# Attention step of a fused attention and MLP kernel: score matmuls placed around the output matmuls

## The chip, the cores and the metric

One core of a Trainium2 chip runs the whole program as a single launch. The metric is device time in microseconds (us): the median of three runs, 599.78 us before the change, with the runs between 599.56 and 600.16 us.

## The reference: what is computed

Chunked attention on 4 batches x 8 heads x 768 positions with a head size of 64, followed by a two-layer MLP on the 3072 rows of 512 that it gives. The core of it, cut:

```python
for c in range(nc):                       # chunks of 32 queries
    l_start, r_end = max(0, c*32 - 16), min(S, c*32 + 32 + 8)
    k_full = concat([mem_k, k[:, :, l_start:r_end]])     # 8 memory keys + window
    v_full = concat([mem_v, v[:, :, l_start:r_end]])
    a = softmax(q_c @ k_full.T / 8)
    out[:, :, chunk] = a @ v_full
x = out.transpose(0, 2, 1, 3).reshape(3072, 512)
h = x @ w_in                              # 512 -> 2048
g = max(h, 0) + alpha * min(h, 0)
return g @ w_out                          # 2048 -> 512
```

All of it is float32. The large products are made exact enough by splitting each operand into a high and a low part and doing three matmuls (low x high, high x low, high x high).

## The kernel before

**The MLP.** The 3072 rows are cut into seven blocks, the first four of 384 rows and the last three of 512. For each block and each of 16 slices f of the hidden layer, an *up* step (L723, 12 matmuls) fills one of two PSUM banks, `h0` or `h1` in turn. ScalarE (L732) and VectorE (L735 `bend`, L741, L745) then turn that bank into the high and low parts of g. A *down* step (L753) later adds the slice into the block's output banks. These up and down steps are nearly all of the work of PE, the engine of the matmuls.

**The attention.** A unit is a pair of heads of one batch over half of the sequence; there are 32. Units 0 to 7 are done by other code at the start. Units 8 to 31 are done in twelve pairs, spread over the MLP. The list `BEGIN` names the place (the number of the MLP slice) at which each pair starts: 20, 26, 31, 36, 42, 47, 53, 57, 63, 71, 79, 87. At each such place `attend` issues on PE

- the *outputs* of the pair before (`olds`): `value_products` (L438), 8 matmuls a unit, on the transposed weights `pt` and on `v_t`; a float32 matmul stands in the trace as two records, so 32 for a pair;
- the *scores* of the pair that begins (`news`): `head_products` (L337), 24 matmuls a unit, 96 records for a pair, in tiles of 64x32.

The scores of both new units lie in two banks, `s0` for the first heads and `s1` for the second heads; each bank holds columns of both units. When a bank is complete, VectorE masks it (L347 or L349), takes row maxima over both units at once (L360) and negates them (L363). ScalarE then does the exponentials (L371). Later VectorE transposes the weights into `pt` (L413), which the outputs of this pair will read one place later.

The outputs of a unit lie in one bank. `bank(u)` gives `a` to even units and `h1` to odd units below 24, but `h0` to even and `h1` to odd units from 24 to 29. From there ScalarE copies the high part (`xh`, L474) and VectorE computes the low part (`xl`, L477), which also sets the bank free. So an up step that comes next in `h0` or `h1` waits until VectorE has done `xl` of the unit that lay there.

**What sets the order.** Nothing is scheduled on the chip: each engine takes its instructions in the order in which the program holds them. That order is made when the program is built, by a planner (`Plan.send`). Each piece of work is a *step* with an engine, an assumed cost, the keys that it reads and writes (banks, tiles), and a due time. The planner runs a list schedule over them and emits each step's instructions when its turn comes. The assumed costs thus decide the order on all engines, and nothing else; waits on the chip come from real dependences.

Of the kernel before, what the change touches and what calls it, by code (L numbers as in the profile page):

```python
# [70 lines left out]
PE, DVE, ACT, POOL, SP = "PE", "DVE", "ACT", "POOL", "SP"  # L71
# [110 lines left out]
def body(ctx: ExitStack, tc: tile.TileContext, qvw, kw, first, w_in, w_out, alpha, out):  # L182
    nc = tc.nc
    ctx.enter_context(tc.manual_schedule())
    NKB, NPT, NA = 2, 2, 2
# [20 lines left out]
    qk = [const.tile([P, BT + NT * NKT], F32, name=f"qk{i}") for i in range(NKB)]  # L206
# [21 lines left out]
    step = plan.add  # L228
# [20 lines left out]
    def rest(place):  # L249
        wide = NNARROW * NF  # L250
        return (len(ORDER) - max(place, wide)) * WIDE_PAIR + max(wide - place, 0) * PAIR
# [9 lines left out]
    def sets(u):  # L261

        return u % NKB
# [55 lines left out]
    def banks(us):  # L319

        n = len(us)
        ss = [ps_s.tile([P, 512], F32, name="s_ps", tag=f"s{h2}")[:, :n * NJ * KW].rearrange("p (u n k) -> p u n k", u=n, n=NJ)
              for h2 in range(2)]
        for i, u in enumerate(us):
            state[u]["s"] = [s[:, i] for s in ss]
        state[us[0]]["all"] = ss

    def head_products(u):

        st = state[u]  # L330
        for n in range(NJ):
            for g in range(4):
                t, j = SLOT[(g, n)]
                c = t * NJ + j
                for h2 in range(2):
                    rows = slice(h2 * D, (h2 + 1) * D)
                    nc.tensor.matmul(  # L337
                        out=st["s"][h2][g * CH:(g + 1) * CH, n],
                        lhsT=qs[sets(u)][rows, c * CH:(c + 1) * CH],
                        rhs=kbs[sets(u)][rows, t, STARTS[j]:STARTS[j] + KW],  # L340
                        start=True, stop=True,
                    )
# [39 lines left out]
    def weights(u):  # L382
# [12 lines left out]
        def spread():  # L395
# [7 lines left out]
    TURNS = [(g, j, n0, n1, t0) + piece  # L403
             for g in range(4)
             for j, n0, n1, t0 in ([(g, 0, NJ, 0)] if g < NJ else [(n, n, n + 1, NT - 1) for n in range(NJ)])
             for piece in PIECES[j]]
# [15 lines left out]
    def bank(u):  # L422


        h2 = u % 2
        if u >= NU - 2:
            return ps_s, f"s{h2}", ("s", h2)
        if h2 or u >= 6 * NPAIR:
            return ps_h, f"h{h2}", f"h{h2}"
        return ps_a, "a", "a"  # L430

    def value_products(u):
        st = state[u]
        pool, tag, _ = bank(u)
        st["a"] = pool.tile([P, 512], F32, name="a_ps", tag=tag)
        for t in range(NT):
            for h2 in range(2):
                nc.tensor.matmul(  # L438
                    out=st["a"][h2 * D:(h2 + 1) * D, t * TQ:(t + 1) * TQ],
                    lhsT=st["v"][:, t, h2, :],  # L440
                    rhs=pts[u % NPT][:, :, t, h2, :],
                    start=True, stop=True,
                )

    def attend(place, olds, news):

        def outputs():
            for u in olds:
                value_products(u)

        def products():
            banks(news)
            for u in news:
                head_products(u)

        due_at = place + (0 if (olds + news)[-1] < FIRST_FRONT else 0.8 if news else -0.3)
        if olds:
            step(PE, 0.2 + 0.53 * len(olds), outputs,
                 reads=[x for u in olds for x in [("v", u % 2)] + [("pt", u % NPT, i) for i in range(len(TURNS))]],
                 writes=[bank(u)[2] for u in olds], rest=rest(due_at))  # L460
        if news:
            step(PE, 0.11 + 0.48 * len(news), products, reads=[(x, sets(u)) for u in news for x in "qk"],
                 writes=[("s", 0), ("s", 1)], rest=rest(due_at + 0.01))

    def split(u, ak="a"):

# [404 lines left out]
    for blk, f in ORDER:  # L871
        if blk == 0:
            decode(f)
        f0, f1 = (0, NF) if blk != 1 else (0, NJOINT) if f < NJOINT else (NJOINT, NF)
        add_up, add_bend, add_down = hidden(blk, f, f0, f1 - 1)
        add_up()
        if down is not None:
            down()
        if done is not None:
            done()  # L880
            done = None
        add_bend()
        now = todo.get(PLACE[blk, f], [])
        olds, news = ([u for u, part in now if part == which] for which in (2, 0))
        if olds or news:
            attend(PLACE[blk, f], olds, news)
        for u in olds:
            split(u, bank(u)[2])
            if u + 2 < NU:
                load_v(u + 2)  # L890
        for u, part in now:
            if part == 1:
                weights(u)
                turn(u)
        for u in news:
            unit_begins(u)
        o = o_ps.setdefault((blk, f1), [])
        down = partial(add_down, o)
        if f == f1 - 1:
            done = partial(keep if f1 < NF else store, blk, o)  # L900
# [57 lines left out]
```

## Time and profile before

| | |
|---|---|
| median of three runs | 599.78 us |
| lowest, highest | 599.56, 600.16 us |
| profiled execution: span from first to last instruction | 597.5 us |
| PE busy | 591.1 us (99%) |
| VectorE (DVE) busy | 386.7 us (65%) |
| ScalarE (ACT) busy | 210.6 us (35%) |
| granted TensorE clock | 1.000 |

The profiled execution is known by its span; its own time with what lies around the span is not recorded, and the median of the runs lies 2.3 us above the span. In the profile PE is the matmul row, PEld the weight loads of the same engine, DVE is VectorE and ACT is ScalarE. A line such as L337 is a line of the kernel before.

### The profile page before, as it was taken

Reading aid. Unit: us, or ns where it says so; the run is one execution under the profiler, and the core shown is the slowest. Engines: PE = TensorE matmul, PEld = TensorE weight load, DVE = VectorE, ACT = ScalarE, POOL = GpSimd, SP = SyncE. Lnnn points to the kernel's source line nnn. Section 1 sums busy time; section 2 is a strip of 40 time slices with the busy share of each in tenths; the row PEclk is TensorE's granted clock in tenths of the full one; section 3 lists DMA queues with packets and bytes.
Section 4 is the critical chain, followed back from the end, with each engine's and each line's share of the span. In section 5 each row is a group of like instructions: output and inputs, shape, how many; then the busy total and the mean of one; then the engine's idle time right before and its main releaser. Section 6 shows DMA issues by size and latency. Waiting matters only on the chain.

```text
span 597.5 us, 10975 instructions
## 1 busy us (share of the span) xinstructions
PE 591.1 (99%) x4430; PEld 505.7 (85%) x4430; DVE 386.7 (65%) x904; ACT 210.6 (35%) x580; POOL 36.5 (6%) x61
## 2 busy tenths in 40 slices
PE   8999999999999999999999999999999999999997
PEld 4789999888998989989898888888888888888885
DVE  5888898887959768685885852861862771530530
ACT  3788888644222504323233302302400411210201
POOL 3510000010001101010010100100100100000000
PEclk9999999999999999999999999999999999999999
DMA  8999500222040302403304003003101000000001
GB/s 337 359 399 407 226 0 1 66 65 89 2 152 2 101 23 79 153 1 100 94 8 150 4 1 100 2 0 109 62 2 36 1 0 36 36 1 0 1 1 71
DMA packets 21076, 48.96 MB, mean 82 GB/s; under 512 B 2464, under 2 KB 5792, under 8 KB 21024
## 3 DMA queue, kind: packets, MB, share of 16 engines
q1 hardware_dynamic: 20880, 48.12, 22.8%
q8 instruction: 35, 0.57, 0.4%
q14 instruction: 17, 0.14, 0.1%
q10 hardware_dynamic: 144, 0.13, 0.1%
HBM read 41.95 MB, written 6.29 MB: 81 GB/s over the span
## 4 chain that ended last, share of the span: by engine, by line
PE 96%; DMA 3%; SPq 0%; ACT 0%; issue 0%; ACTq 0%
PE h_ps L723 45%; PE o_ps L753 44%; PE a_ps L438 3%; DMA early<-first 3%; PE s_ps L337 2%; PE a_ps L559 1%; PE o_ps L546 1%; PE s_ps L312 0%; SPq L490 0%; PE o_ps L298 0%; ACT o_t L810 0%; PE s_ps L298 0%; ACTq L810 0%
## 5 line engine op out<-in xcount | busy, mean ns | idle before, releaser
L723 PE MATMUL h_ps<-xh,w 128*128 128x384 f32 (+1 forms) x896 | 248.8, 358 | 0.0
L723 PEld LDWEIGHTS h_ps<-xh,w 128*128 128x128 f32 x896 | 164.9, 188 | 16.0
L753 PE MATMUL o_ps<-w,gh 128*128 128x512 f32 x528 | 162.7, 389 | 0.0
L723 PE MATMUL h_ps<-xl,w 128*128 128x384 f32 (+1 forms) x448 | 162.6, 363 | 0.0
L732 ACT ACTIVATE g<-h_ps 128x384 f32<-128x384 f32 (+1 forms) x112 | 60.4, 540 | 194.7 <-PE h_ps L723 129.1
L735 DVE SCALAR_TENSOR_TENSOR g<-g,rise,h_ps 128x384 f32<-128x384 f32 (+1 forms) x112 | 74.7, 668 | 74.8 <-ACT g L732 74.1
L753 PEld LDWEIGHTS o_ps<-w,gh 128*128 128x128 f32 x528 | 99.1, 188 | 20.4
L413 DVE STREAM_TRANSPOSE pt<-e 32x64 f32<-32x64 f32 (+1 forms) x336 | 99.4, 301 | 7.4 <-POOL e L392 2.0
L753 PE MATMUL o_ps<-w,gl 128*128 128x512 f32 x264 | 102.8, 389 | 0.0
L723 PEld LDWEIGHTS h_ps<-xl,w 128*128 128x128 f32 x448 | 84.1, 188 | 10.2
L753 PE MATMUL o_ps<-w,xh 128*128 128x512 f32 x240 | 74.8, 393 | 0.0
L753 PEld LDWEIGHTS o_ps<-w,gl 128*128 128x128 f32 x264 | 49.6, 188 | 10.2
L477 DVE TENSOR_TENSOR xl<-a_ps,xh 128x384 fp32r<-128x384 f32 x32 | 17.6, 554 | 61.0 <-ACT xh L474 60.4
L753 PEld LDWEIGHTS o_ps<-w,xh 128*128 128x128 f32 x240 | 45.0, 188 | 8.9
L741 DVE CAST gh<-g 128x512 fp32r<-128x512 f32 (+1 forms) x72 | 28.8, 401 | 30.6 <-PE o_ps L753 28.2
L474 ACT CAST xh<-a_ps 128x384 fp32r<-128x384 f32 x32 | 15.0, 483 | 95.0 <-PE a_ps L438 93.7
L392 POOL TENSOR_TENSOR e<-e,den 128x384 f32<-128x384 f32 x24 | 22.8, 949 | 419.6 <-DVE den L389 270.0
L745 DVE TENSOR_TENSOR gl<-g,gh 128x512 fp32r<-128x512 f32 (+1 forms) x72 | 46.6, 648 | 1.7
L371 ACT ACTIVATE e<-s_ps,mx 128x64 f32<-128x64 f32 x144 | 43.4, 318 | 11.1 <-DVE mx L363 11.1
L753 PE MATMUL o_ps<-w,xl 128*128 128x512 f32 x120 | 46.8, 390 | 0.0
L371 ACT ACTIVATION_READ_ACCUMULATOR e<-s_ps,mx 128x1 f32 x144 | 30.4, 211 | 0.0
L810 ACT COPY o_t<-o_ps 128x512 f32<-128x512 f32 x21 | 12.2, 591 | 44.6 <-PE o_ps L753 44.2
(58 smaller groups left out, 380.2 us busy)
## 6 DMA issues: line engine op xcount, KB each, us to landing
w_t<-w_in SPq DMA_DIRECT2D x16, 512.0 KB, 10.0
w_t<-w_out SPq DMA_DIRECT2D x16, 512.0 KB, 10.1
qk<-kw SPq DMA_DIRECT2D x24, 272.0 KB, 4.3
v_t<-qvw SPq DMA_DIRECT2D x24, 256.0 KB, 2.8
out<-o_t SPq DMA_DIRECT2D x23, 256.0 KB, 2.1
early<-first SPq DMA_DIRECT2D x8, 656.0 KB, 6.2
qk<-qvw SPq DMA_DIRECT2D x24, 192.0 KB, 4.8
early<-first SPq DMA_DIRECT2D x8, 256.0 KB, 6.3
```

The source lines that it names most:

```text
L371: nc.scalar.activation(out=st["e"][:, i], in_=st["s"][h2][:, n], func=AF.Exp, scale=SCALE, bias=d["mx"][:, u - us[0], n, h2:h2 + 1], accum ...
L392: nc.gpsimd.tensor_tensor(out=st["e"], in0=st["e"], in1=st["den"].broadcast_to([P, NJ * 2, KW]), op=ALU.mult)
L413: nc.vector.transpose(out=pts[u % NPT][quad * CH:(quad + 1) * CH, j, t0:t0 + n1 - n0].rearrange("p t h q -> p (t h) q"), in_=(st["e"], zer ...
L438: nc.tensor.matmul(out=st["a"][h2 * D:(h2 + 1) * D, t * TQ:(t + 1) * TQ], lhsT=st["v"][:, t, h2, :], rhs=pts[u % NPT][:, :, t, h2, :], sta ...
L474: nc.scalar.copy(out=ring[k][0][:, cols], in_=st["a"][:, :BT])
L477: nc.vector.tensor_tensor(out=ring[k][1][:, cols], in0=st["a"][:, :BT], in1=ring[k][0][:, cols].bitcast(F32), op=ALU.subtract)
L723: nc.tensor.matmul(out=h["ps"][:, :n_cols], lhsT=ws[f, 0][:, wk, k * P:(k + 1) * P], rhs=parts(blk, k)[1](xk), start=(k == 0 and n == 0), ...
L732: nc.scalar.activation(out=h["g"], in_=h["ps"][:, :n_cols], func=AF.Relu, scale=-1.0)
L735: nc.vector.scalar_tensor_tensor(out=h["g"], in0=h["g"], scalar=rise[:, f:f + 1], in1=h["ps"][:, :n_cols], op0=ALU.mult, op1=ALU.add)
L741: copy(out=h["gh"], in_=h["g"])
L745: nc.vector.tensor_tensor(out=h["gl"], in0=h["g"], in1=h["gh"].bitcast(F32), op=ALU.subtract)
L753: nc.tensor.matmul(out=o_ps[tt], lhsT=h[gk][:, tt * P:(tt + 1) * P], rhs=ws[f, 1][:, wk], start=(f == first_f and i == 0), stop=(f == last ...
```

## The change

In a step that has both older and new units, outputs and scores were two separate planner steps. They become one step, `around`: scores of the first new unit, outputs of both older units, scores of the second new unit. The step reads and writes what both read and wrote. The assumed costs change too: 2.66 us for the joint step where the two had 1.26 and 1.07 us, and 1.68 and 1.27 us for outputs or scores that stand alone. Eleven places have such a joint step (all of `BEGIN` but the first); the first pair's scores and the last pair's outputs stay alone.

```diff
-        def products():
-            banks(news)
-            for u in news:
+        def products(us):
+            if us[0] == news[0]:
+                banks(news)
+            for u in us:
                 head_products(u)
+        def around():
+            products(news[:1])
+            outputs()
+            products(news[1:])
...
+        if olds and len(news) > 1:
+            step(PE, 1.0 + 0.83 * len(olds), around, reads=fed + asked, writes=made + scored, rest=rest(due_at))
+            return
         if olds:
-            step(PE, 0.2 + 0.53 * len(olds), outputs, ... rest=rest(due_at))
+            step(PE, 0.2 + 0.74 * len(olds), outputs, reads=fed, writes=made, rest=rest(due_at))
         if news:
-            step(PE, 0.11 + 0.48 * len(news), products, ... rest=rest(due_at + 0.01))
+            step(PE, 0.11 + 0.58 * len(news), partial(products, news), reads=asked, writes=scored, rest=rest(due_at + 0.01))
```

In the changed kernel the lines behind `attend` have numbers higher by 9: L477 becomes L486, L723 becomes L732, L753 becomes L762.

What it makes of the order, at three places. First PE at place 71, the first of three places (71, 79 and 87) whose outputs lie in `h0` and `h1`. `s_ps` are the scores, `a_ps` the outputs, `h_ps` the bank of the up step that follows; the words behind a row name the engines for whose semaphores it waits. Before:

```order
L753 MATMUL o_ps<-w,gh 128x512 x2
L438 MATMUL a_ps<-pt_634,v_t 64x96 [waits DMAHW7_49]
L438 MATMUL a_ps<-pt_634,v_t 64x96 x7
L438 MATMUL a_ps<-pt_636,v_t 64x96 [waits DMAHW0_49]
L438 MATMUL a_ps<-pt_636,v_t 64x96 x7
L337 MATMUL s_ps<-qk_154 32x64 x22
L337 MATMUL s_ps<-qk_155 32x64 [waits DMAHW4_49,DMAHW2_49]
L337 MATMUL s_ps<-qk_155 32x64 x23
L723 MATMUL h_ps<-xl,w 128x512 [waits DVE_49]
```

and now:

```order
L762 MATMUL o_ps<-w,gh 128x512 x2
L337 MATMUL s_ps<-qk_154 32x64 x22
L438 MATMUL a_ps<-pt_634,v_t 64x96 [waits DMAHW2_49]
L438 MATMUL a_ps<-pt_634,v_t 64x96 x7
L438 MATMUL a_ps<-pt_636,v_t 64x96 [waits DMAHW3_49]
L438 MATMUL a_ps<-pt_636,v_t 64x96 x7
L337 MATMUL s_ps<-qk_155 32x64 [waits DMAHW5_49,DMAHW1_49]
L337 MATMUL s_ps<-qk_155 32x64 x23
L732 MATMUL h_ps<-xl,w 128x512 [waits DVE_49,PE_49]
```

One unit's scores moved ahead of the outputs; between the outputs and the up step there is now one unit's scores instead of two. Second, VectorE at the same place (`MEMSET s_ps` is the mask, `TENSOR_REDUCE mx` the maxima, `xl<-a_ps` what sets `h0` and `h1` free). Before, and then now:

```order
L745 TENSOR_TENSOR gl<-g,gh 128x512
L477 TENSOR_TENSOR xl<-a_ps,xh 128x384 x2
L347 MEMSET s_ps 32x2x16
L360 TENSOR_REDUCE mx<-s_ps 128x6
L363 TENSOR_SCALAR mx<-mx 128x12
```

```order
L754 TENSOR_TENSOR gl<-g,gh 128x512
L347 MEMSET s_ps 32x2x16
L360 TENSOR_REDUCE mx<-s_ps 128x6
L486 TENSOR_TENSOR xl<-a_ps,xh 128x384 x2
L363 TENSOR_SCALAR mx<-mx 128x12
```

The mask and the maxima of the first score bank moved ahead of both `xl`. (The second bank's mask and maxima stand behind the `xl` rows in both, and their rows would read like the first's.) In the planner both are ready at the end of the one joint step, and the maxima have the earlier due time. Third, PE at place 26, where the two parts stood apart: before, the scores went first and the outputs came 18 us later, with up and down steps between.

```order
L337 MATMUL s_ps<-qk_154 32x64 x24
L337 MATMUL s_ps<-qk_155 32x64 x24
L723 MATMUL h_ps<-xl,w 128x384
...
L438 MATMUL a_ps<-pt_634,v_t 64x96 x8
L438 MATMUL a_ps<-pt_636,v_t 64x96 x8
```

```order
L337 MATMUL s_ps<-qk_154 32x64 x24
L438 MATMUL a_ps<-pt_634,v_t 64x96 x8
L438 MATMUL a_ps<-pt_636,v_t 64x96 x8
L337 MATMUL s_ps<-qk_155 32x64 x24
L762 MATMUL o_ps<-w,xl 128x512
```

The scores moved back to where the outputs stand, and the loads of the next pair's keys and queries on SyncE's queue with them. The same holds for place 57; at place 36 scores and outputs stood together with the scores first, and at the other eight places with the outputs first.

More of the change, by code (lines that the diff above doesn't have):

```diff
@@ L449, in outputs @@
                 value_products(u)
-        def products():
-            banks(news)
-            for u in news:
+        def products(us):
+            if us[0] == news[0]:
+                banks(news)
+            for u in us:
                 head_products(u)
+        def around():
+            products(news[:1])
+            outputs()
+            products(news[1:])
         due_at = place + (0 if (olds + news)[-1] < FIRST_FRONT else 0.8 if news else -0.3)
+        fed = [x for u in olds for x in [("v", u % 2)] + [("pt", u % NPT, i) for i in range(len(TURNS))]]
+        asked = [(x, sets(u)) for u in news for x in "qk"]
+        made, scored = [bank(u)[2] for u in olds], [("s", 0), ("s", 1)]
+        if olds and len(news) > 1:
+            step(PE, 1.0 + 0.83 * len(olds), around, reads=fed + asked, writes=made + scored, rest=rest(due_at))
+            return
         if olds:
-            step(PE, 0.2 + 0.53 * len(olds), outputs,
-                 reads=[x for u in olds for x in [("v", u % 2)] + [("pt", u % NPT, i) for i in range(len(TURNS))]],
-                 writes=[bank(u)[2] for u in olds], rest=rest(due_at))
+            step(PE, 0.2 + 0.74 * len(olds), outputs, reads=fed, writes=made, rest=rest(due_at))
         if news:
-            step(PE, 0.11 + 0.48 * len(news), products, reads=[(x, sets(u)) for u in news for x in "qk"],
-                 writes=[("s", 0), ("s", 1)], rest=rest(due_at + 0.01))
+            step(PE, 0.11 + 0.58 * len(news), partial(products, news), reads=asked, writes=scored, rest=rest(due_at + 0.01))
     def split(u, ak="a"):
```

## The prediction

> **What bounds the kernel.** I read the busy table and the chain first, then PE's waits, then the stages. The first fence is from the page: busy time by engine, and the chain that ended last. The second lists everything that PE waited for.
>
> ```profile
> PE 591.1 (99%) x4430; PEld 505.7 (85%) x4430; DVE 386.7 (65%) x904; ACT 210.6 (35%) x580; POOL 36.5 (6%) x61
> PE 96%; DMA 3%; SPq 0%; ACT 0%; issue 0%; ACTq 0%
> ```
>
> ```profile
> PE s_ps L298 <- DVE warm L224: 1.5, 1, 1.5
> PE a_ps L559 <- DMA early<-first: 0.4, 1, 0.4
> PE s_ps L298 <- DVE e L513: 0.4, 1, 0.4
> PE s_ps L312 <- DMA early<-first: 0.2, 1, 0.2
> ```
>
> PE is the whole chain, and its only waits lie in the first microseconds. So every change of PE's own time, and every wait that the change gives to PE, goes straight into the end. Nothing can be won by taking waits away, since there are none. By stage (length, then busy time of PE, PEld, DVE, ACT, POOL, clock, DMA):
>
> ```profile
> 120.00:330.00 210.00, 210.00 (x1965) 188.02 (x1964) 159.12 (x450) 69.86 (x282) 14.85 (x16) 1.00 0.23 73
> 330.00:505.00 175.00, 175.00 (x1144) 144.73 (x1143) 97.70 (x241) 38.35 (x129) 7.91 (x8) 1.00 0.08 27
> ```
>
> The eight earlier joint steps lie in the first of these, where VectorE is 76% busy; the last three lie in the second, at 56%.
>
> **Part 1: the matmuls themselves.** Place 71 in PE's timeline (start, length, what): down steps, then 32 records of outputs, 96 of scores, then the up step. Below it, the line of the score matmuls (duration min/median/max).
>
> ```profile
> 365.12 0.61 PE L753 MATMUL o_ps<-w,gh 128*128 128x512 f32 x2
> 365.66 1.54 PE L438 MATMUL a_ps<-pt,v_t 128*64 128x96 f32 x32
> 367.13 1.24 PE L337 MATMUL s_ps<-qk 64*32 64x64 f32 x96
> 368.30 0.50 PE L723 MATMUL h_ps<-xl,w 128*128 128x512 f32 x1
> 368.64 0.63 PE L723 MATMUL h_ps<-xh,w 128*128 128x512 f32 x2
> 369.11 0.40 PE L723 MATMUL h_ps<-xl,w 128*128 128x512 f32 x1
> ```
>
> ```profile
> L337 PE MATMUL s_ps<-qk x1152: 212/216/241, 111.1 to 461.0; 64*32 64x64 f32 x192
> ```
>
> Start to start, the outputs hold PE for 367.13 - 365.66 = 1.47 us and the scores for 368.30 - 367.13 = 1.17 us. The last score matmul starts 1.24 - 0.216 = 1.02 us after the first, so 1.17 - 1.02 = 0.15 us is a tail: the next form of matmul starts that much after the last of this one, where score matmuls follow one another at 1.02 / 95 = 0.011 us. One half of the scores then costs 0.51 + 0.15 = 0.66 us, and two halves 1.32 where the whole costs 1.17: a split adds 0.15 us. Entering a run of small matmuls costs too. Large matmuls follow at 0.23 (two of them from 368.64 to 369.11), so the second of the down pair starts at 365.35 and the outputs 0.31 after it: some 0.09 more. And the first up matmul behind the run is followed after 0.34 (368.30 to 368.64) instead of 0.23: 0.11 more. A run that stands alone pays these 0.20 us by itself.
>
> Does the order of the two matter? Place 36 has scores first:
>
> ```profile
> 193.13 1.24 PE L337 MATMUL s_ps<-qk 64*32 64x64 f32 x96
> 194.31 1.54 PE L438 MATMUL a_ps<-pt,v_t 128*64 128x96 f32 x32
> 195.78 0.44 PE L723 MATMUL h_ps<-xl,w 128*128 128x384 f32 x1
> ```
>
> 1.18 and 1.47 us: the same blocks either way. And the two places (26 and 57) where they stood apart; here 57:
>
> ```profile
> 291.34 1.24 PE L337 MATMUL s_ps<-qk 64*32 64x64 f32 x96
> 292.51 0.44 PE L723 MATMUL h_ps<-xl,w 128*128 128x384 f32 x1
> 294.82 1.54 PE L438 MATMUL a_ps<-pt,v_t 128*64 128x96 f32 x32
> ```
>
> Two runs, two times 0.20 us of entry and exit. So nine places go from one run of 1.47 + 1.17 to one of 0.66 + 1.47 + 0.66: 9 x 0.15 = +1.35. Two places lose one entry and exit and gain one split: 2 x (0.15 - 0.20) = -0.10. Sum of part 1: **+1.25 us**. Its bounds: a split can cost nothing if the tail is swallowed (then 11 x 0 - 2 x 0.20 = -0.4), and at most twice the tail if the output run also slows by as much (+2.9). I take the middle value because the trace has exactly these neighbours, scores then outputs and outputs then scores, at fixed cost.
>
> The Trainium skill has a rule that reads against this term. In "TensorE: Matmul & The Clock Gate", section "The mechanism", weight loads that go to other rows of the array are pulled ahead of running matmuls, which would hide the second unit's loads under the outputs and make the split free: the sum below would be near 603.4 us. The page "TensorEngine Tiling (Array Packing)", section "Key Properties", says instead that a change of tiling mode drains the engine. The trace stands with the second: the 0.15 us tail.
>
> **Part 2: the bank `h0`.** At places 71, 79 and 87 the outputs of the even unit lie in `h0`, and the next up step writes `h0`. It must wait for that unit's `xl`. VectorE's and ScalarE's rows at place 71:
>
> ```profile
> 366.59 0.48 ACT L474 CAST xh<-a_ps 128x384 fp32r<-128x384 f32 x1 [15.30 <-PE a_ps L438]
> 367.10 1.22 DVE L477 TENSOR_TENSOR xl<-a_ps,xh 128x384 fp32r<-128x384 f32 x2 [11.06 <-ACT xh L474]
> 368.43 0.09 DVE L347 MEMSET s_ps<- 32x32 f32 x1
> 368.55 0.56 DVE L360 TENSOR_REDUCE mx<-s_ps 128x6 f32<-128x384 f32 x1
> 369.10 0.09 DVE L347 MEMSET s_ps<- 32x32 f32 x1
> ```
>
> Before, the first `xl` ended about 367.66, 0.64 us ahead of the up step at 368.30, so nothing waited. Now the mask and maxima of the first score bank stand ahead of it on VectorE, and they need the scores of both units. Call the start of the outputs t. The second unit's scores start at t + 1.47; their last matmul at t + 1.98. The mask came 368.43 - (367.13 + 1.02) = 0.28 us after the last score matmul: t + 2.26. From mask to `xl` place 47 has the very sequence, mask, maxima, `xl`:
>
> ```profile
> 247.08 0.09 DVE L347 MEMSET s_ps<- 32x32 f32 x1
> 247.20 0.56 DVE L360 TENSOR_REDUCE mx<-s_ps 128x6 f32<-128x384 f32 x1
> 247.68 0.55 DVE L477 TENSOR_TENSOR xl<-a_ps,xh 128x384 fp32r<-128x384 f32 x1
> ```
>
> 0.60 us to the start of `xl`, 0.55 for it: it ends at t + 3.41. How soon PE follows a VectorE instruction shows only at the start of the program:
>
> ```profile
> 8.43 0.55 DVE L513 TENSOR_TENSOR e<-s_ps,mx 128x384 f32<-128x384 f32 x1
> 9.03 0.11 PEld L298 LDWEIGHTS <-busy 128*128 128x128 bf16 x2 [0.22 <-DVE e L513]
> ```
>
> 0.05 us. The up step could start at t + 3.46; PE reaches it at t + 1.47 + 0.66 = t + 2.13. The wait is **1.33 us**, three times: **+4.0 us**. Nothing else is on PE to fill it, since PE takes its instructions in order and the up step is the next. The clock stays at 1.00 in the row of the stage, and the wait of 1.5 us at the start left it there, so I give the wait no further price. What bounds this term: 1.23 (the longer step behind the run, 0.11 us, is swallowed by the wait) and 1.43 (the second bank's mask started 0.67 us after the first in the rows of place 71, not 0.60, and the same again for spread). At the other eight places the bank is `a` and `h1`. There the step behind is a down step of some 2 us, or an up step in `h0`, and the planner put the `xl` of `h1` first; it ends at t + 3.4, while PE reaches `h1` at t + 2.13 plus at least three quarter steps of 0.52 us (a step takes 2.09, below): t + 3.7. No wait, but only 0.3 us to spare.
>
> **Part 3: what becomes late.** The outputs need `pt`. The last transposes before places 36 and 47, the outputs of 47, then what lies between the outputs of place 53 and those of place 57 (294.82, above):
>
> ```profile
> 193.21 1.00 DVE L413 STREAM_TRANSPOSE pt<-e 32x64 f32<-32x64 f32 x4
> 242.98 1.00 DVE L413 STREAM_TRANSPOSE pt<-e 32x64 f32<-32x64 f32 x4
> 244.31 1.54 PE L438 MATMUL a_ps<-pt,v_t 128*64 128x96 f32 x32
> 248.93 0.17 DVE L363 TENSOR_SCALAR mx<-mx 128x12 f32<-128x12 f32 x1
> ...
> 271.95 1.54 PE L438 MATMUL a_ps<-pt,v_t 128*64 128x96 f32 x32
> 274.60 0.44 PE L723 MATMUL h_ps<-xl,w 128*128 128x384 f32 x1
> 292.81 0.74 DVE L413 STREAM_TRANSPOSE pt<-e 32x64 f32<-32x64 f32 x3
> ```
>
> Transposes ended 0.3 us before the outputs at place 47 (243.98), and 0.1 us at place 36 (194.21 against 194.31). Two shifts meet here. One unit's scores now stand ahead, so outputs start 0.66 us later against the start of the joint step. And the chain of a pair, maxima to transposes, starts with the second unit's scores; the negation that ends its first part came at t + 4.6 (248.93) and now, with mask at t + 2.26 and the same four instructions behind it, again near t + 4.6. Place 57 is the closest that I find. Its transposes ended at 293.55, 21.6 us after the outputs of place 53. Its outputs now start 2.13 + 16.7 (274.60 to 291.34, eight up and down steps, 2.09 each) + 2.2 (the up step that stood between scores and outputs, 292.51 to 294.82) + 0.66 = 21.7 us after them: 0.1 us to spare. I take nothing for this, and up to 0.5 us at three places as the upper end.
>
> Place 26's loads of keys and queries move by 18 us on SyncE's queue. They still have the ten steps to place 31 to land, some 21 us, and take 4.8:
>
> ```profile
> qk<-qvw SPq DMA_DIRECT2D x24, 192.0 KB, 4.8
> ```
>
> The softmax work that moves with them is VectorE's, which has 24% of this stage free; without that cover it is the late rival below.
>
> **The sum.** 1.25 + 4.0 = +5.2 us on a span of 597.5: 602.7 us. The 2.3 us between span and median stay, so 599.78 + 5.2 = **605.0 us**, 0.9% slower.
>
> **The rivals.**
> - *The queue fills under the outputs.* 32 of the 96 score matmuls fall in the first quarter microsecond (the row counts them):
>
> ```profile
> 222.22:222.47 0.25, 0.24 (x32) 0.25 (x33) 1.00 0.00 0
> ```
>
>   The other 64 take 1.02 - 0.25 = 0.77, 0.012 each. If the quick start is a queue filled while slower work ran, each half would have it: 0.25 + 16 x 0.012 = 0.44 instead of 0.51, which gives back 22 x 0.07 = 1.5 us: 603.5. Against it: grouped rows don't tell whether the first half of a whole run was quicker than the second, and if both took 0.51 the quick start is no matter of a queue that stood full. The Trainium skill gives TensorE a queue of 64 instructions ("Advanced Engine Details and Errata", "Engine Queue Depths"), which the 32 matmuls and 33 loads of this row fit.
> - *VectorE becomes late in the stage 120 to 330.* Places 47 and 57, and the up steps in `h1`, have 0.1 to 0.3 us to spare; three misses of 0.5 us give +1.5: 606.5.
> - *No wait for `h0`.* If the up step were released by `xh` alone, only part 1 stays: 601.0. Against it stands the wait on VectorE in the order of the up step.
> - *Not slower.* The score halves would have to run so fast that both terms are repaid: 5.2 / 22 = 0.24 us less each, 0.27 us for 48 matmuls, 5.7 ns each. The fastest stretch shows 0.25 / 32 = 7.8 ns. At 5 ns a half takes 0.24 and the time is 599.1; the point from which it decides is 5.7 ns.
>
> **Chances.** My forecast (604.2 to 605.9) 0.60, the queue 0.15, VectorE late 0.13, no wait 0.08, not slower 0.04. The range holds all but the last and what lies beyond: from 600.9 to 607.0. A change within 0.2% (1.2 us) can't be told from none; half of "no wait" and half of "not slower" fall there. So faster 0.03, same 0.06, slower 0.91.
>
> **What would show it.** Right: PE's waits list three waits of 1.2 to 1.4 us of the up step's `h_ps` on VectorE's `xl`, at places 71, 79 and 87; each joint run holds PE 2.79 us from its first score to the next step; the scores' line stays at 0.216 us a matmul. Wrong: no PE wait there; the second half's matmuls closer than the first's; waits of the outputs on transposes.

## The result, and the profile after

The changed kernel takes 605.19 us (median of four runs, 604.96 to 605.48) against 599.71 us for the kernel before: ratio 1.0092, 95% interval 1.0077 to 1.0106. It is 5.5 us slower; 605.0 us was forecast. The span of the profiled execution went from 597.5 to 603.3 us.

The page of the kernel after, busy time and chain; then the three largest entries of PE's waits (the two left out are 0.4 us each, at the program's start):

```profile
PE 592.4 (98%) x4430; PEld 506.4 (84%) x4430; DVE 387.0 (64%) x904; ACT 211.2 (35%) x580; POOL 35.7 (6%) x61
PE 96%; DMA 3%; DVE 1%; SPq 0%; issue 0%; ACT 0%; ACTq 0%
```

```profile
PE h_ps L732 <- DVE xl L486: 4.0, 3, 1.3
PE s_ps L298 <- DVE warm L224: 1.5, 1, 1.5
PE s_ps L312 <- DMA early<-first: 0.7, 3, 0.3
```

The first row of the waits is new: the up step's bank `h_ps` waited for `xl` three times, 4.0 us in all. VectorE is now 1% of the chain, where it had no part. PE's busy time rose by 1.3 us. The two together make 5.3 of the 5.5 us. Where the wait lies, at place 71, on PE, then ScalarE, then VectorE (start, length, what, idle time before it and what ended that):

```profile
367.00 0.72 PE L337 MATMUL s_ps<-qk 64*32 64x64 f32 x48
367.65 1.54 PE L438 MATMUL a_ps<-pt,v_t 128*64 128x96 f32 x32
369.12 0.72 PE L337 MATMUL s_ps<-qk 64*32 64x64 f32 x48
371.19 0.47 PE L732 MATMUL h_ps<-xl,w 128*128 128x512 f32 x1 [1.34 <-DVE xl L486]
```

```profile
368.58 0.48 ACT L483 CAST xh<-a_ps 128x384 fp32r<-128x384 f32 x1 [15.95 <-PE a_ps L438]
```

```profile
369.90 0.09 DVE L347 MEMSET s_ps<- 32x32 f32 x1 [12.53 <-PE s_ps L337]
370.02 0.56 DVE L360 TENSOR_REDUCE mx<-s_ps 128x6 f32<-128x384 f32 x1
370.50 1.01 DVE L486 TENSOR_TENSOR xl<-a_ps,xh 128x384 fp32r<-128x384 f32 x2
```

ScalarE had the high part of `h0` done at 369.06. VectorE, idle for 12.53 us, still did nothing with it: the mask stands ahead in its queue and waits for the second unit's scores, which end after 369.8. `xl` starts at 370.50, 1.4 us after it could have, and PE stands from about 369.85 to 371.19.

How much of the 5.5 us lies in which stage is read from starts of PE's rows. First the scores of the first pair before the change, then after:

```profile
111.14 1.24 PE L337 MATMUL s_ps<-qk 64*32 64x64 f32 x96
```

```profile
111.57 1.24 PE L337 MATMUL s_ps<-qk 64*32 64x64 f32 x96
```

From there to the run at place 71 it took 365.66 - 111.14 = 254.52 us before and 367.00 - 111.57 = 255.43 after: +0.9 us for the eight earlier places. The 0.43 us is the start of the program, up to these first scores, where the change leaves PE's and SyncE's order as it was (over all profiles here these scores start between 111.1 and 112.5). The rest is what comes from place 71 on: 603.3 - 367.00 = 236.3 us against 597.5 - 365.66 = 231.8, so 4.5 us for the last three places. Without the start that is 0.9 + 4.5 = 5.4 us, as in the medians. The last three places' stage by the windows view (length, busy PE, PEld, DVE, ACT, POOL, clock, DMA, GB/s) has PE idle for 180.00 - 175.97 = 4.0 us, at full clock:

```profile
330.00:510.00 180.00, 175.97 (x1146) 145.25 (x1145) 99.06 (x243) 39.20 (x136) 7.68 (x8) 1.00 0.09 26
```

### The profile page after: what moved, and what is told of

It reads as the page before. It is cut to its first block, busy times and chain, and to the rows that moved or that the text cites. A ratio compares the mean times of both kernels' runs of the same rounds, so it can differ in the third digit from the quotient of the medians.

```text
span 603.3 us, 10984 instructions
## 1 busy us (share of the span) xinstructions
PE 592.4 (98%) x4430; PEld 506.4 (84%) x4430; DVE 387.0 (64%) x904; ACT 211.2 (35%) x580; POOL 35.7 (6%) x61
## 4 chain that ended last, share of the span: by engine, by line
PE 96%; DMA 3%; DVE 1%; SPq 0%; issue 0%; ACT 0%; ACTq 0%
PE h_ps L732 44%; PE o_ps L762 44%; PE a_ps L438 3%; DMA early<-first 3%; PE s_ps L337 3%; PE a_ps L568 1%; PE o_ps L555 1%; PE s_ps L312 0%; DVE mx L360 0%; SPq L499 0%; DVE xl L486 0%; PE o_ps L298 0%; ACT o_t L819 0%; PE s_ps L298 0%; DVE s_ps L349 0%
## 5 line engine op out<-in xcount | busy, mean ns | idle before, releaser
L732 PE MATMUL h_ps<-xh,w 128*128 128x384 f32 (+1 forms) x896 | 248.9, 359 | 0.0
L732 PEld LDWEIGHTS h_ps<-xh,w 128*128 128x128 f32 x896 | 164.9, 188 | 16.2
L732 PE MATMUL h_ps<-xl,w 128*128 128x384 f32 (+1 forms) x448 | 162.0, 362 | 4.0 <-DVE xl L486 4.0
L762 PE MATMUL o_ps<-w,gh 128*128 128x512 f32 x528 | 162.8, 390 | 0.0
L762 PEld LDWEIGHTS o_ps<-w,gh 128*128 128x128 f32 x528 | 99.1, 188 | 20.4
L762 PE MATMUL o_ps<-w,gl 128*128 128x512 f32 x264 | 103.1, 390 | 0.0
L732 PEld LDWEIGHTS h_ps<-xl,w 128*128 128x128 f32 x448 | 84.1, 188 | 14.3 <-issue 4.4
L762 PE MATMUL o_ps<-w,xh 128*128 128x512 f32 x240 | 74.8, 393 | 0.0
L762 PEld LDWEIGHTS o_ps<-w,gl 128*128 128x128 f32 x264 | 49.6, 188 | 10.4
L762 PEld LDWEIGHTS o_ps<-w,xh 128*128 128x128 f32 x240 | 45.0, 188 | 8.8
L762 PE MATMUL o_ps<-w,xl 128*128 128x512 f32 x120 | 46.9, 391 | 0.0
L762 PEld LDWEIGHTS o_ps<-w,xl 128*128 128x128 f32 x120 | 22.5, 188 | 4.3
```

Of the source, the lines that this page charges most:

```text
L732: nc.tensor.matmul(out=h["ps"][:, :n_cols], lhsT=ws[f, 0][:, wk, k * P:(k + 1) * P], rhs=parts(blk, k)[1](xk), start=(k == 0 and n == 0), ...
L762: nc.tensor.matmul(out=o_ps[tt], lhsT=h[gk][:, tt * P:(tt + 1) * P], rhs=ws[f, 1][:, wk], start=(f == first_f and i == 0), stop=(f == last ...
```

## The experiments

The wait, the split of the scores, the joint step and the assumed costs come together in this change. The first eight runs take them apart; the last two follow something that turned up on the way. Medians are compared with runs of the kernel before on the same chip.

| run | median us | before us | ratio, 95% interval |
|---|---|---|---|
| low parts ahead of the maxima | 601.22 | 599.80 | 1.0022 (1.0013 to 1.0031) |
| joint step up to place 63 alone | 601.07 | 599.80 | 1.0021 (1.0012 to 1.0029) |
| joint step at 71, 79, 87 alone | 604.46 | 599.80 | 1.0076 (1.0063 to 1.0090) |
| joint, unsplit | 603.46 | 599.80 | 1.0064 (1.0051 to 1.0076) |
| joint, scores first | 601.44 | 599.64 | 1.0029 (1.0017 to 1.0040) |
| unsplit, low parts ahead | 599.55 | 599.64 | 0.9997 (0.9988 to 1.0006) |
| assumed costs alone | 600.31 | 599.64 | 1.0009 (1.0000 to 1.0018) |
| maxima twice | 608.40 | 599.64 | 1.0145 (1.0132 to 1.0159) |
| maxima three times | 612.54 | 600.18 | 1.0210 (1.0193 to 1.0227) |
| maxima five times | 618.24 | 600.18 | 1.0298 (1.0282 to 1.0313) |

**Low parts ahead of the maxima.** In the planner the maxima now also depend on the older units' low parts, at the last three places:

```diff
+        freed = [("xl", u % NPAIR, AT[u % NPAIR][u // NPAIR]) for u in (us[0] - 2, us[0] - 1) if 24 <= u < 30]
         for h2 in range(2):
-            step(DVE, ..., partial(top, h2), writes=[("s", h2), mk], ...)
+            step(DVE, ..., partial(top, h2), reads=freed, writes=[("s", h2), mk], ...)
```

> The changed kernel, but at places 71, 79 and 87 the low parts of the older units (which set h0 and h1 free) stand ahead of the score maxima on VectorE again; PE's order is that of the changed kernel. Theory (the three waits come from VectorE's order): xl of h0 ends near t + 2.0, the up step comes at t + 2.13, so no wait is left, and 3 x 1.39 = 4.2 us go: 601.0 us, +1.2 over before. Rival (the shorter cover behind the outputs is itself too short, the up step waits for ScalarE's copy and xl anyway): waits of 0.3 us or more stay, 602 us or above.

601.22 us. PE at place 71, then VectorE:

```profile
369.41 0.72 PE L337 MATMUL s_ps<-qk 64*32 64x64 f32 x48
370.06 0.51 PE L733 MATMUL h_ps<-xl,w 128*128 128x512 f32 x1
```

```profile
369.38 1.22 DVE L487 TENSOR_TENSOR xl<-a_ps,xh 128x384 fp32r<-128x384 f32 x2 [11.71 <-ACT xh L484]
370.59 0.09 DVE L347 MEMSET s_ps<- 32x32 f32 x1
```

The same matmuls in the same order, and the up step starts 0.65 us after the second unit's scores, with no wait. `xl` ran while the scores did. The wait thus comes from VectorE's order; 4.0 us went with it.

**The joint step at part of the places.** One condition each (`news[0] < 26` or `>= 26`); where it doesn't hold, two steps with the old assumed costs.

> The joint step at the eight places up to 63 alone; at 71, 79 and 87 outputs and scores are two steps with the old assumed costs. Theory: six splits at 0.138 us and two merged runs that save 0.066 us each, +0.7: 600.4 us, no wait on PE. Rival (the moved softmax work makes VectorE late in this stage, or the other order there costs by itself): 601.5 us or above, with waits of the outputs or up steps on VectorE.

> The joint step at places 71, 79 and 87 alone; the order up to place 63 is that of the kernel before. Theory: three splits at 0.138 and three waits of 1.39 us net, +4.6: 604.3 us. Rival (the stage before has a larger share): 603 us or below.

604.46 us for the last three places alone, +4.7, where the theory had +4.6. The eight earlier places alone took 601.07 us, between theory (600.4) and rival (601.5), so this forecast was missed. The rival's sign is absent: PE's waits show neither transposes nor `xl`. From the first scores (111.39) to the outputs at place 71 (366.78) it took 255.39 us, +0.9 over before, as in the changed kernel:

```profile
111.39 1.24 PE L337 MATMUL s_ps<-qk 64*32 64x64 f32 x96
366.78 1.54 PE L438 MATMUL a_ps<-pt,v_t 128*64 128x96 f32 x32
```

So 0.9 us is inside the stage, where 0.7 was worked out, and 0.4 of the +1.27 in the medians lies outside it. In this trace the first scores start 0.25 us later than before, and from the issue of the last store to the end of the span it takes some 0.4 us longer (595.44 to 598.9, before 594.40 to 597.5). That is one execution, quicker than the median of its run; whether the same makes the medians differ is not shown.

**Joint, but unsplit.**

```diff
         def around():
-            products(news[:1])
             outputs()
-            products(news[1:])
+            products(news)
```

> One joint step at all eleven places, but outputs of both older units first and then the scores of both new ones, unsplit. Theory: no split, two merged runs save 0.2 us each (-0.4); the maxima still stand ahead of xl at the last three places, so the up step there comes at t + 3.97 instead of t + 2.64, three waits of 1.3 us (+4.0): 603.3 us. Rival A (the split is free and all of the loss is waits): same as the changed kernel, 605.2 us. Rival B (the wait needs the split, since only then the second unit's scores come late): 599.3 us.

603.46 us, where the theory had 603.3, with the waits of the changed kernel:

```profile
PE h_ps L731 <- DVE xl L485: 4.0, 3, 1.3
```

Rival A (the split is free) and rival B (the wait needs the split) both fall. The wait needs only that the planner sees outputs and scores end together. It then counts the maxima as ready at that moment and the low parts one ScalarE copy later, and sends the maxima first. (The part on the change, ahead of the prediction, put this down to an earlier due time. By the planner's code only steps that are ready are compared, so the readiness decides.)

**Joint, scores first.** `around` is `products(news)`, then `outputs()`.

> One joint step at all eleven places, unsplit, with the scores of both new units first and then the outputs. Theory (the wait is set by how late VectorE gets to xl of h0): the scores end before the outputs start, so mask and maxima of the first bank are done before ScalarE's copy of h0 is (t + 1.41); xl ends near t + 2.0, the up step comes at t + 2.1 where PE would be there at t + 1.47: three waits of 0.6 us. No split, two merged runs: -0.25. Sum 601.4 us. Rival (the wait goes with the maxima standing ahead of xl, as in the changed kernel, whatever the place of the scores): three waits of 1.3 us, 603.5 us.

601.44 us. PE's wait, its rows at place 71, then VectorE's:

```profile
PE h_ps L731 <- DVE xl L485: 1.5, 3, 0.5
```

```profile
367.28 1.54 PE L438 MATMUL a_ps<-pt,v_t 128*64 128x96 f32 x32
369.33 0.50 PE L731 MATMUL h_ps<-xl,w 128*128 128x512 f32 x1 [0.51 <-DVE xl L485]
```

```profile
367.52 0.56 DVE L360 TENSOR_REDUCE mx<-s_ps 128x6 f32<-128x384 f32 x1
368.72 1.22 DVE L485 TENSOR_TENSOR xl<-a_ps,xh 128x384 fp32r<-128x384 f32 x2 [0.64 <-ACT xh L482]
```

Now the maxima stand ahead of `xl` and do no harm: they are over at 368.08, and `xl` waits for ScalarE's copy instead. What is left, 0.5 us each, is the plain chain from outputs to a free bank with no scores behind the outputs to cover it.

**Unsplit, low parts ahead.** The edits of the first and the fourth run together.

> One joint step, outputs first and then all scores, and at the last three places the low parts ahead of the maxima on VectorE. Theory: no split and no wait; only the two merged runs remain: 599.5 us, 0.25 below before; it lies 11 x 0.14 = 1.5 us below the run that has the same VectorE order with split scores (601.2). Rival (the split is free): 601.2 us like that run.

599.55 us, no wait. From its first scores (111.38) to place 71 (365.62) it took 254.24 us, 0.3 less than before:

```profile
111.38 1.24 PE L337 MATMUL s_ps<-qk 64*32 64x64 f32 x96
365.62 1.54 PE L439 MATMUL a_ps<-pt,v_t 128*64 128x96 f32 x32
```

Relative to before it stands at -0.09 us, the split run with the same VectorE order at +1.42: 1.5 us for eleven splits, 0.14 each. This version beats the changed kernel, and can't be told from the kernel before (interval 0.9988 to 1.0006). It is the best found.

**The assumed costs alone.** `around` is never used; the costs 1.68 and 1.27 stay.

> Two separate planner steps at every place as before, with the new assumed costs (1.68 and 1.27 us) alone. The order moves in the stage up to place 63 (three places instead of two have scores and outputs apart), not at the last three. Theory: PE work the same, one more run with its own entry, no wait: 599.9 us. Rival (the costs carry part of the loss by the order that they make): 600.4 us or above.

600.31 us, +0.67, with an interval that begins at 1.0000: inconclusive. Its trace shows no wait of an up step or of outputs, but its first scores only at 112.27, 1.1 us later than in the trace of before; at the program's start PE waited 1.4 us for loads where it had waited 0.2:

```profile
PE s_ps L312 <- DMA early<-first: 1.4, 4, 0.7
```

Between there and the end it is within 0.1 us of before. Whether the costs move the medians through the start was not tried further.

**The maxima twice.**

```diff
-            nc.vector.tensor_reduce(out=d["mx"][:, :, :, h2], in_=s, ...)
+            for _ in range(2 if h2 == 0 and 26 <= us[0] else 1):
+                nc.vector.tensor_reduce(out=d["mx"][:, :, :, h2], in_=s, ...)
```

> The changed kernel, with the maxima of the first score bank taken twice at places 71, 79 and 87 (the result is the same); PE's order is that of the changed kernel. Theory (VectorE's queue ahead of xl is the wait): one more maxima instruction of 0.5 to 0.6 us in each wait, 1.34 becomes 1.9, +1.6 over the changed kernel: 606.8 us. Rival (the wait ends with something else, such as ScalarE's copy or the end of the scores): no change, 605.2 us.

```profile
PE h_ps L733 <- DVE xl L487: 5.8, 3, 1.9
```

Each wait grew by 0.6 us, as the theory had it, so VectorE's queue is the wait. But the time is 608.40, not 606.8. The missing 1.6 us lie behind the third wait. PE there, then the windows around it (length, busy times, clock third from the end):

```profile
468.97 0.47 PE L733 MATMUL h_ps<-xl,w 128*128 128x512 f32 x1 [1.94 <-DVE xl L487]
...
470.64 0.63 PE L733 MATMUL h_ps<-xl,w 128*128 128x512 f32 x1
471.07 1.06 PE L733 MATMUL h_ps<-xh,w 128*128 128x512 f32 x2
```

```profile
468.00:470.10 2.10, 1.13 (x5) 0.99 (x6) 2.02 (x6) 0.00 (x0) 0.00 (x0) 1.00 0.28 102
470.15:473.55 3.40, 3.40 (x9) 2.68 (x9) 0.02 (x1) 1.10 (x7) 0.00 (x0) 0.50 0.00 0
473.60:477.00 3.40, 3.40 (x16) 2.81 (x15) 2.21 (x6) 2.32 (x12) 0.51 (x1) 1.00 0.00 0
```

Matmuls follow one another at 0.43 us there (470.64 to 471.07) instead of 0.23. For 3.4 us the granted clock was 0.50, and as many microseconds later held 16 matmuls where these held 9.

**Three times and five times.** To see whether the low clock belongs to the length of the wait.

> As the run with the maxima twice, with the maxima three times: each of the three waits 0.6 us longer again, 1.94 becomes 2.54. That run took 608.4 us, 1.4 more than its waits explain, and its trace shows a clock of 0.54 to 0.61 for 3.4 us behind the third wait. Theory (a wait can cost a stretch of low clock of its own, the likelier the longer it is): waits give 608.8 us, and two or three of them are followed by a stretch of about 3.4 us at half clock that costs 1.6 us: 612 to 613.6 us. Rival (the low clock came from something else at that place, not from the length of the wait): one stretch or none, behind the third wait only: 608.8 to 610.4 us.

> The maxima five times: waits of 3.74 us, the waits alone give 612.4 us. Theory: a low-clock stretch behind each of the three waits, 617.2 us. Rival: one stretch or none, 612.4 to 614.0 us.

Three times: PE's wait, and windows behind the first, second and third of them.

```profile
PE h_ps L733 <- DVE xl L487: 7.6, 3, 2.5
```

```profile
373.20:376.60 3.40, 3.40 (x9) 2.64 (x8) 0.20 (x2) 1.00 (x6) 0.00 (x0) 0.50 0.55 203
424.40:427.80 3.40, 3.40 (x9) 2.65 (x8) 0.00 (x0) 1.13 (x8) 0.00 (x0) 0.50 0.74 263
474.00:478.00 4.00, 4.00 (x19) 3.29 (x18) 1.45 (x4) 2.27 (x13) 0.00 (x0) 1.00 0.00 0
```

Five times, with two rows for the first wait, whose low clock began before the wait ended:

```profile
PE h_ps L733 <- DVE xl L487: 11.1, 3, 3.7
```

```profile
370.00:374.00 4.00, 0.29 (x3) 0.30 (x2) 3.75 (x8) 0.00 (x0) 0.00 (x0) 0.75 0.69 205
374.00:378.00 4.00, 4.00 (x10) 3.13 (x10) 0.86 (x4) 1.00 (x6) 0.00 (x0) 0.50 0.30 108
426.50:430.00 3.50, 3.50 (x9) 2.71 (x10) 1.00 (x4) 1.29 (x8) 0.00 (x0) 0.51 0.76 272
477.70:481.20 3.50, 2.97 (x7) 2.44 (x8) 1.66 (x5) 1.00 (x6) 0.00 (x0) 0.51 0.00 0
```

612.54 and 618.24 us: the theory's 612 to 613.6 and, 1.0 us over it, 617.2 (the first of its stretches was a double one). In the profiled executions, of the three waits in each run those of 1.3 us (the changed kernel) were followed by a low clock in no case, those of 1.9 in one, of 2.5 in two, of 3.7 in all three. The rival, that the place of the third wait is to blame, falls: with three maxima that place alone stays at full clock.

## Why the prediction was right

- **What bounds the kernel.** That PE is the whole chain and each wait goes straight into the end held: 4.0 us of waits and about 1.3 us of PE's own time make 5.3 of the 5.5 us.
- **Part 1, the matmuls (+1.25).** Measured +0.9 up to place 63. For the last three places, three splits at the measured 0.14 us add 0.4: +1.3. The half of the scores holds PE 0.65 us (367.65 - 367.00; 0.66 was worked out). The middle value was right against both bounds. By parts it was a little less exact: for the eight early places the term's own prices give 6 x 0.15 - 0.10 = 0.8 against 0.9.
- **The rule against this term.** Between the two pages of the Trainium skill, "TensorE: Matmul & The Clock Gate" (loads pulled ahead, section "The mechanism") and "TensorEngine Tiling (Array Packing)" (a change of mode drains, section "Key Properties"), the runs side with the second for this kernel: a split is not free, it costs 0.14 us, by the unsplit run. That a drain is what takes this time no run shows.
- **Part 2, the bank `h0` (+4.0).** Measured 1.34 us a wait where 1.33 was worked out, at the three places named and nowhere else. In starts it is 371.19 - 369.12 = 2.07 us from the second half of the scores to the up step, against 0.65 without the wait in the run with the low parts ahead: 1.42, of which a few hundredths come back at the first up matmul, which is followed after 0.31 instead of 0.35 (371.19 to 371.50; 370.06 to 370.41). The 1.33 was worked out in starts, so 1.42 is the figure to set beside it: the mechanism was right, the size lay at the upper bound (1.43), and the match with the 1.34 of the waits view, which counts from the modelled end of the last score matmul, is closer than the working earned. What was too small is the step from VectorE to PE, taken as 0.05 us from the start of the program: the first `xl` started at 370.50 and took 0.55, so it ended 0.14 us ahead of the up step.
- **Part 3, what becomes late (0).** No wait appeared. Place 57, counted at 0.1 us to spare, had 0.5: transposes end at 294.76, the outputs start at 295.30. (The working took 2.2 us for a step that its own rows, 292.51 to 294.82, give as 2.3; the rest is that the transposes came earlier than assumed.)

```profile
294.01 0.75 DVE L413 STREAM_TRANSPOSE pt<-e 32x64 f32<-32x64 f32 x3
```

```profile
295.30 1.54 PE L438 MATMUL a_ps<-pt,v_t 128*64 128x96 f32 x32
```

- **The queue rival.** Each half does begin with some 32 records in 0.24 us, but the 16 behind them take 0.27 and not the 0.19 that the rival had: 0.51 us in all. The first half of a whole run before the change took the same 0.51, so the split gave nothing back.
- **The clock.** "I give the wait no further price" held for waits of 1.3 us, but its two reasons don't carry it. The stage with a clock of 1.00 had no waits in it. And the wait of 1.5 us at the start did not leave the clock at 1.00: the eight matmuls behind it took 3.48 us, 0.43 us each, where two of the same kind soon after took 0.61 us together. 0.43 us is the pace that 128x512 matmuls keep in the stretches of half clock above, so by this pace the clock was low there, though the windows view shows 1.00. Nothing in the traces before told how long a wait may be, and at 1.9 us a low stretch did follow one, for 1.6 us more. That 1.3 us cost nothing more came out right without a reason in the trace: luck.

```profile
1.46 3.48 PE L298 MATMUL s_ps<-busy 128*128 128x512 bf16 x8 [1.46 <-DVE warm L224]
5.72 0.61 PE L298 MATMUL s_ps<-busy 128*128 128x512 bf16 x2
```

- **The sum.** "The 2.3 us between span and median stay" did not hold: after the change it is 605.19 - 603.3 = 1.9, and in every run for which both span and time are on record it is 1.7 to 1.9. The profiled execution before was therefore probably some 0.5 us quicker than its median, which is why the spans differ by 5.8 us and the medians by 5.5. The forecast of 605.0 starts from the median before and does not hang on it; the forecast span of 602.7 was 0.6 us short.

The cause of the 4 us is shown from five sides: the wait goes when VectorE's order is put back (601.22), stays without the split (603.46), shrinks when the scores come first (601.44), comes alone with the last three places (604.46), and grows by what is put ahead of `xl` (1.3, 1.9, 2.5 us). The other 1.3 us go with the splits: without them, and without the waits, the time is that of the kernel before (599.55). Open is the 0.4 to 0.6 us by which medians of kernels with nearly the same inner stages differ.

## What to carry to other kernels

Joining two pieces of work on the bottleneck engine also joins them in the scheduler's eyes, and the engines behind it can then get another order: look there first, at which instruction frees the bank that the bottleneck needs next, and what stands ahead of it. Interleaving small matmuls of another shape has a price that a trace gives at once, the gap where the shapes change (0.15 us here) against the gap inside (0.01 us). And a wait on TensorE that is short by itself can be followed by a stretch at half clock, so a wait of two microseconds can cost more than it shows.

## What the runs showed of the hardware that was not expected

After some waits of 1.94 us and more TensorE's granted clock fell to 0.50, mostly for one stretch of 3.4 us (once, at the first wait of 3.7 us, for two such stretches). One stretch costs about 1.6 us: 3.4 us in which 9 large matmuls were started where 16 fit at full clock.

Which of several equal waits is followed by one is not a matter of length alone. By the windows view the stretches of one run begin whole numbers of 3.41 us apart, at 373.17 and 424.37 with the maxima three times (15 x 3.41) and at 371.98, 426.60 and 477.80 with five (16 and 15 x 3.41). By these figures the clock is set in windows of 3.41 us that run on whatever the kernel does, and a wait falls into one window or across two. The windows that hold the larger part of each wait, first with the maxima twice, then three times (length, then busy time of PE; what is missing is the wait):

```profile
367.75:371.16 3.41, 2.24 (x91) 1.92 (x80) 1.04 (x3) 0.96 (x2) 0.00 (x0) 1.00 0.36 92
418.95:422.36 3.41, 1.91 (x8) 1.61 (x9) 2.59 (x7) 1.11 (x6) 0.00 (x0) 1.00 0.83 252
466.74:470.15 3.41, 1.48 (x25) 1.17 (x19) 2.90 (x8) 0.16 (x1) 0.00 (x0) 1.00 0.49 153
```

```profile
369.76:373.17 3.41, 0.93 (x4) 0.83 (x5) 3.27 (x8) 0.00 (x0) 0.00 (x0) 1.00 0.59 155
420.96:424.37 3.41, 1.43 (x6) 1.23 (x7) 3.03 (x8) 0.63 (x2) 0.00 (x0) 1.00 0.79 245
472.16:475.57 3.41, 1.89 (x8) 1.61 (x9) 2.61 (x7) 0.60 (x5) 0.00 (x0) 1.00 0.17 64
```

The third, fourth and fifth row hold 1.93, 2.48 and 1.98 us of wait, and the window behind each of them is at half clock. The others hold 1.17, 1.50 and 1.52, and full clock follows. With five maxima the windows ahead of the three stretches hold 1.96 us and more; the changed kernel has at most its whole 1.34 us in one window. In these traces the bound thus lies between 1.5 and 1.9 us of wait in one window. This is read from one trace of each run afterwards; no run was made to move a wait within its window.

The Trainium skill ("TensorE: Matmul & The Clock Gate", section "What's actually happening") has a free-running window of about 3.4 us and a throttle after an idle one. The window and the stretch agree; the idle time doesn't, since 1.93 us of wait in a window of 3.41 was enough here. The small matmuls of the joint run did not count as idle: the first row, 367.75 to 371.16, holds 2.24 us of them (the joint run lasts from 367.14 to 369.99), no large matmul and 1.17 us of wait, and full clock follows it.
